# The second products' weight tiles 64 bytes further on in SBUF, in a fused attention and gated feed-forward kernel

## Chip, cores and metric

One NeuronCore of a Trainium2 chip runs the whole program. The metric is the device time of one execution in microseconds; a kernel's time is the median of several executions.

## The reference

Inputs are q, k, v of shape 8 x 8 x 576 x 64 (batch, heads, positions, head size) and three weight matrices. Attention is the sum of a coarse part (q, k, v averaged over groups of four positions, full softmax over 144 groups) and a band part (each position sees those at a distance under four). The result, seen as x of 4608 tokens by 512, goes through a normalisation and a gated feed-forward layer:

```python
rms = np.sqrt(np.mean(x * x, axis=-1, keepdims=True) + 1e-06)
xn = x / rms * rms_g
g = xn @ w_gate                         # 512 x 1536
silu = g * (1.0 / (1.0 + np.exp(-g)))
val = xn @ w_val                        # 512 x 1536
return (silu * val @ w_out)             # 1536 x 512
```

Everything is float32.

## The kernel before

The tokens are worked in 18 chunks (`c`) of 256. For every chunk the class `Attention` makes x: VectorE forms the band scores and most of the sums, ScalarE and GpSimd some of the products with v. `squares`, `mean`, `rms` and `root` give 1/rms, `norm` scales x, and `turn`, `high`, `low` turn it with TensorE and split it into `xh` (float32r) and the rest `xl`. The class `Coarse` does the coarse part for one pair of heads at a time, on TensorE too, spread over the program.

The class `Forward` does the feed-forward layer for a chunk, in 12 blocks `f` of 128 columns of w_gate and w_val. Weights too are kept as a float32r tile and its rest (`wg`, `wv`, `wo`, two of each), and each product is the sum of three: high by high, and high by rest both ways.

- `first(f, 0)` and `first(f, 1)` (L975) are 12 matmuls each. The stationary operand is a 128 x 128 piece of `wg` or `wv`, the moving operand 256 columns of `xh` or `xl`.
- `tanh`, `gate`, `product`, `high`, `low` turn the two results into `hs[f]` (its high part and its rest, each 256 wide).
- `second(f)` (L1010) is 6 matmuls that add to two output tiles. The stationary operand is a 128 x 128 piece of `hs`, the moving operand one block of `wo`, 512 columns. It follows `first` by `LAG` = 2 blocks.

So a block is 24 matmuls of 256 columns and 6 of 512; 18 x 12 blocks make 5184 and 1296 of them. Each matmul loads its stationary operand anew, and this load runs beside the matmul ahead of it.

All weights stay in SBUF in tiles of the pool `const`. Chunks 0 to 2, their weights, and the opening are put in order by a planner (`Plan`) with costs and due times; from chunk 3 on the program's order is written out in the loop at the end, and the tile framework lays the engines' queues out from it.

The tiles of one pool lie behind each other in the partition, in the order in which they are first asked for. Each weight class asks for its parts by need: `first_place` (blocks 0 to 7, which also serve as the first landing place of q, k and v sums), and `raw_place` (the last four blocks, as landing places of raw weights). The small tiles `z_b` (sums of the softmax, 64 bytes in a partition), `ss` (sums of squares, 32 bytes) and `rinv` (1/rms, 32 bytes) come from the pool `band`, two buffers each.

Of the kernel before, what the change touches and what calls it, by code (L numbers as in the profile page):

```python
# [8 lines left out]
FP32 = mybir.dt.float32  # L9
# [10 lines left out]
P = 128  # L20
# [13 lines left out]
US = 4  # L34
# [136 lines left out]
def attn_moe_kernel(  # L171
# [18 lines left out]
    const = ctx.enter_context(tc.tile_pool(name="const", bufs=1))  # L190
    stage = ctx.enter_context(tc.tile_pool(name="stage", bufs=1))
    loads = ctx.enter_context(tc.tile_pool(name="loads", bufs=2))
    band = ctx.enter_context(tc.tile_pool(name="band", bufs=2))
# [42 lines left out]
    wg = [Weight(f"wg{i}", [KT, P], [0, NF - 4, NF]) for i in range(2)]  # L236
    wv = [Weight(f"wv{i}", [KT, P], [0, NF - 4, NF]) for i in range(2)]
    wo = [Weight(f"wo{i}", [DM], [0, NF - 4, NF - 2, NF]) for i in range(2)]

# [343 lines left out]
    class Attention:  # L585
# [54 lines left out]
        def plan(self, newton="POOL", before=()):  # L640
# [69 lines left out]

            up_ready = [stored[b, hp] for p_ in {(2 * c + j) // UPP for j in range(2)} for b in (2 * p_, 2 * p_ + 1) for hp in range(KT)]
            squares, adds = [], []
            for j in range(2):
                load = task("ACT", 0.12, lambda j=j: self.load_up(j), T - 30, up_ready, allocs=[ups[j]], lag=2.5)
# [6 lines left out]
            self.added = adds  # L721
            mp = buf("ps_a")
            mean = task("PE", 0.2, self.mean, T - 10 - TAIL, squares, allocs=[mp])
            rms = task("DVE", 0.48, self.rms, T - 10, [mean], allocs=[r], uses=[mp])
            root = task(newton, 2.6 if newton == "POOL" else 1.9, lambda: self.root(newton), T - 10, [rms], uses=[r])
# [58 lines left out]
            nc.scalar.activation(out=self.f, in_=self.f, func=AF.Exp, scale=0.125)  # L784

        def total(self):
            self.z = band.tile([P, 4 * US], FP32, name="z_b")
            nc.vector.tensor_reduce(out=self.z, in_=self.f, axis=AX.X, op=ALU.add)

        def invert(self):  # L790
# [58 lines left out]

        def squares(self, j):  # L850
            if j == 0:
                self.ss = band.tile([P, 2 * US], FP32, name="ss")
            x = self.x[j].rearrange("p s t d -> p s (t d)")
            for s in range(US):
                nc.scalar.activation(
                    out=self.up[j].rearrange("p t d -> p (t d)"), in_=x[:, s], func=AF.Square,
                    accum_out=self.ss[:, j * US + s:j * US + s + 1],
                )
# [5 lines left out]
        def rms(self):  # L864
            self.r = band.tile([P, 2 * US], FP32, name="rms", bufs=1)
            nc.vector.tensor_scalar(
                out=self.r, in0=self.rp, scalar1=1.0 / DM, scalar2=1e-6, op0=ALU.mult, op1=ALU.add,
            )
            self.inv = band.tile([P, 2 * US], FP32, name="rinv")
            nc.vector.tensor_scalar(  # L870
                out=self.inv.bitcast(U32), in0=self.r.bitcast(U32), scalar1=1, scalar2=None, op0=ALU.logical_shift_right,
            )
            yi = self.inv.bitcast(U32)
            nc.vector.tensor_scalar(
                out=yi, in0=yi, scalar1=-1, scalar2=0x5F3759DF, op0=ALU.mult, op1=ALU.add,
            )
# [149 lines left out]
    for fg in range(3):  # L1026
        for i in range(12):
            if i % 3 == 2 if fg < 2 else i >= 8:
                f = 4 * fg + (i // 3 if fg < 2 else i - 8)
# [173 lines left out]
```

## Time and profile before

| | us |
|---|---|
| three timed runs, median | 1148.4 |
| their lowest and highest | 1146.32, 1149.47 |
| the profiled execution | 1145.97 |
| its span from first to last instruction | 1144.2 |
| TensorE busy in the span | 1082.0 |
| VectorE, ScalarE, GpSimd busy | 927.7, 624.1, 255.7 |
| mean granted TensorE clock | 0.977 |

TensorE's matmuls overlap: a matmul's record begins when it starts to stream and ends when its last result is out, so records of one engine lie over each other. How long one really takes from TensorE is the step from one start to the next, and is read from starts. A granted clock of 1.00 is 2.4 GHz, 0.50 is 1.2 GHz.

### The profile page before, as it was taken

What the parts mean: (1) busy time and instruction counts of PE and PEld (TensorE: products, weight loads), DVE (VectorE), ACT (ScalarE), POOL (GpSimd) and SP (SyncE); (2) the same over time, 40 slices, a digit from 0 to 9 for tenths busy, and PEclk for the clock granted to TensorE, in tenths of its full rate; (3) what the DMA queues carried; (4) which work ended last, traced back from release to release, by engine and by line L of the source; (5) the groups of instructions that cost most, each with busy time, mean ns of one, the idle gap of its engine ahead of it and who ended that gap; (6) DMA issues with size and microseconds to landing.
All of it is one profiled execution on the core that took longest, in us unless ns stands there. A gap on an engine that the chain in (4) does not pass through costs nothing.

```text
span 1144.2 us, 22238 instructions
## 1 busy us (share of the span) xinstructions
PE 1082.0 (95%) x8002; PEld 990.2 (87%) x8002; DVE 927.7 (81%) x1869; ACT 624.1 (55%) x2284; POOL 255.7 (22%) x317
## 2 busy tenths in 40 slices
PE   6883799999999899999999999999999999999998
PEld 4772698888899899999999999999999999999997
DVE  6787898778889989797979797979798989887432
ACT  1574673747392847474747474747475573837221
POOL 1554562334221211111111111101011020201000
PEclk9885999999999999999999999999999999999999
DMA  9985482446535353535263535222231313220000
GB/s 264 301 275 170 102 227 76 95 101 149 127 87 117 99 115 88 115 87 115 83 120 87 115 88 114 78 64 75 66 91 46 105 52 99 68 58 20 1 19 19
DMA packets 76815, 119.59 MB, mean 105 GB/s; under 512 B 26784, under 2 KB 36256, under 8 KB 76704
## 3 DMA queue, kind: packets, MB, share of 16 engines
q1 hardware_dynamic: 47520, 97.34, 28.8%
q0 software_dynamic: 8640, 15.93, 9.0%
q10 hardware_dynamic: 20544, 4.89, 2.0%
q8 instruction: 63, 1.03, 0.4%
q14 instruction: 48, 0.39, 0.1%
HBM read 106.33 MB, written 11.80 MB: 103 GB/s over the span
## 4 chain that ended last, share of the span: by engine, by line
PE 76%; DVE 9%; DMA 8%; ACT 3%; issue 3%; SPq 1%; POOL 1%; ACTq 0%; DVEq 0%; POOLq 0%
PE ps_h L975 46%; PE ps_o L1010 23%; PE ps_a L541 2%; DMA wg<-in_v_sum_dram 2%; DMA qk<-in_qk_sum_dram 2%; PE ps_a L499 2%; ACT prod L804 1%; DMA vs<-in_v_sum_dram 1%; PE ps_a L906 1%; DVE prod L757 1%; DVE o_sb L271 1%; PE ps_a L527 1%; DMA kv<-in_k_pad_dram 1%; DVE sc L761 1%; DMA up<-o_g 1%
## 5 line engine op out<-in xcount | busy, mean ns | idle before, releaser
L1010 PE MATMUL ps_o<-wo,hs 128*128 128x512 f32 x1296 | 356.0, 399 | 4.2 <-POOL hs L999 3.7
L975 PE MATMUL ps_h<-xh,wg 128*128 128x256 f32 x1728 | 348.2, 283 | 4.8 <-ACT xh L910 2.3
L975 PE MATMUL ps_h<-xh,wv 128*128 128x256 f32 x1728 | 343.0, 281 | 4.6 <-DVE sil L985 4.5
L975 PEld LDWEIGHTS ps_h<-xh,wg 128*128 128x128 f32 x1728 | 282.9, 190 | 14.2 <-ACT xh L910 3.0
L975 PEld LDWEIGHTS ps_h<-xh,wv 128*128 128x128 f32 x1728 | 281.9, 189 | 10.8 <-DVE sil L985 6.9
L804 ACT ACTIVATE prod<-kv,sc 128x64 f32<-128x64 f32 x1072 | 281.7, 408 | 13.0 <-DVE sc L795 4.8
L1010 PEld LDWEIGHTS ps_o<-wo,hs 128*128 128x128 f32 x1296 | 221.9, 188 | 41.4 <-POOL hs L999 6.2
L975 PE MATMUL ps_h<-xl,wg 128*128 128x256 f32 x864 | 244.8, 283 | 0.1
L975 PE MATMUL ps_h<-xl,wv 128*128 128x256 f32 x864 | 241.5, 280 | 0.0
L982 ACT ACTIVATE sil<-ps_h 128x256 f32<-128x256 f32 x216 | 82.9, 384 | 233.9 <-PE ps_h L975 208.8
L811 POOL TENSOR_TENSOR prod<-sc,kv 128x256 f32<-128x256 f32 x144 | 116.4, 843 | 397.4 <-DVE sc L795 175.4
L985 DVE SCALAR_TENSOR_TENSOR sil<-sil,ps_h 128x256 f32<-128x256 f32 x216 | 89.7, 415 | 103.1 <-ACT sil L982 91.0
L975 PEld LDWEIGHTS ps_h<-xl,wg 128*128 128x128 f32 x864 | 164.1, 190 | 6.9 <-issue 1.3
L975 PEld LDWEIGHTS ps_h<-xl,wv 128*128 128x128 f32 x864 | 163.6, 189 | 1.8
L996 ACT ACTIVATE hs<-sil 128x256 fp32r<-128x256 f32 x216 | 89.5, 416 | 136.9 <-DVE sil L990 122.4
L757 DVE TENSOR_TENSOR prod<-q_t,kv 128x896 f32<-128x896 f32 x140 | 151.7, 1086 | 5.6 <-DMA q_t<-in_q_band_dram 5.2
L830 DVE TENSOR_REDUCE x_t<-prod 128x128 f32<-128x896 f32 x128 | 136.8, 1077 | 23.6 <-ACT prod L804 16.4
L761 DVE TENSOR_REDUCE sc<-prod 128x14 f32<-128x896 f32 x144 | 154.5, 1077 | 0.4
L999 DVE TENSOR_TENSOR hs<-sil,hs 128x256 fp32r<-128x256 f32 x196 | 91.4, 466 | 29.5 <-ACT hs L996 29.2
L990 DVE SCALAR_TENSOR_TENSOR sil<-sil,ps_h 128x256 f32<-128x256 f32 x216 | 89.9, 416 | 8.1 <-PE ps_h L975 6.4
L362 POOL DMA_DIRECT2D qk<-in_qk_sum_dram x36 | 32.2, 895 | 187.3 <-DMA qk<-in_qk_sum_dram 111.8
L811 DVE TENSOR_TENSOR prod<-sc,kv 128x128 f32<-128x128 f32 (+2 forms) x144 | 69.5, 515 | 1.6 <-PE ps_o L826 0.8
(118 smaller groups left out, 984.3 us busy)
## 6 DMA issues: line engine op xcount, KB each, us to landing
kv<-in_k_pad_dram SPq DMA_DIRECT2D x72, 320.0 KB
kv<-in_v_pad_dram SPq DMA_DIRECT2D x72, 320.0 KB
qk<-in_qk_sum_dram POOLq DMA_DIRECT2D x36, 288.0 KB, 5.3
out_dram<-o_sb SPq DMA_DIRECT2D x36, 256.0 KB
q_t<-in_q_band_dram SPq DMA_DIRECT2D x70, 128.0 KB
vs<-in_v_sum_dram POOLq DMA_DIRECT2D x36, 144.0 KB, 3.5
qk<-in_qk_sum_dram SPq DMA_DIRECT2D x12, 288.0 KB
wo<-in_qk_sum_dram SPq DMA_DIRECT2D x2, 1152.0 KB
```

Of the source, the lines that this page charges most:

```text
L757: nc.vector.tensor_tensor(out=pr, in0=bcast(q[:, s0:s0 + 2], 2, NO), in1=window(k, s0), op=ALU.mult)
L761: nc.vector.tensor_reduce(out=self.sc[:, j, par, s0:s0 + 2], in_=self.pr[i], axis=AX.X, op=ALU.add,)
L804: nc.scalar.activation(out=self.pr[i][:, o, s], in_=self.v[j, par][:, s0 + s + o], func=AF.Copy, scale=p[:, s, o:o + 1],)
L811: (nc.vector if engine == "DVE" else nc.gpsimd).tensor_tensor(out=self.pr[i][:, a:b], in0=bcast(p[:, :, a:b].rearrange("p s o -> p o s"), ...
L830: nc.vector.tensor_reduce(out=self.x[j][:, s0:s0 + 2, par], in_=pr.rearrange("p o s d -> p s d o"), axis=AX.X, op=ALU.add,)
L975: nc.tensor.matmul(out=self.p[f][:, t], lhsT=wi(f)[:, 0, k], rhs=xi[:, k], start=(n == 0), stop=(n == 3 * KT - 1),)
L982: nc.scalar.activation(out=self.sil[f], in_=self.p[f][:, 0], func=AF.Tanh, scale=0.5)
L985: nc.vector.scalar_tensor_tensor(out=self.sil[f], in0=self.sil[f], scalar=1.0, in1=self.p[f][:, 0], op0=ALU.add, op1=ALU.mult,)
L990: nc.vector.scalar_tensor_tensor(out=self.sil[f], in0=self.sil[f], scalar=0.5, in1=self.p[f][:, 1], op0=ALU.mult, op1=ALU.mult,)
L996: nc.scalar.activation(out=self.hs[f][:, 0], in_=self.sil[f], func=AF.Copy)
L999: (nc.gpsimd if engine == "POOL" else nc.vector).tensor_tensor(out=self.hs[f][:, 1], in0=self.sil[f], in1=self.hs[f][:, 0], op=ALU.subtract,)
L1010: nc.tensor.matmul(out=self.o[j], lhsT=lhs[:, cols], rhs=rhs(f)[:, 0], start=(f == 0 and i == 0), stop=(f == NF - 1 and i == 2),)
```

## The change

The six small tiles become fixed tiles of the pool `const`, asked for between the weights, so that the weights are now laid out in a written order. Chunk `c` takes number `c % 2` of each, as the two buffers of the pool did.

```diff
+    small = {"ss": [const.tile([P, 2 * US], FP32, name=f"ss{i}") for i in range(2)]}
+    for w in wo:
+        w.first_place()
+    small["inv"] = [const.tile([P, 2 * US], FP32, name=f"rinv{i}") for i in range(2)]
+    for w in wg + wv:
+        w.first_place()
+    for w in wg + wv:
+        w.raw_place(1, 0)
+    small["z"] = [const.tile([P, 4 * US], FP32, name="z_b0")]
+    for k in (1, 2):
+        for w in wo:
+            w.raw_place(k, 0)
+    small["z"].append(const.tile([P, 4 * US], FP32, name="z_b1"))
...
-            self.z = band.tile([P, 4 * US], FP32, name="z_b")
+            self.z = small["z"][self.c % 2]
...
-                self.ss = band.tile([P, 2 * US], FP32, name="ss")
+                self.ss = small["ss"][self.c % 2]
...
-            self.inv = band.tile([P, 2 * US], FP32, name="rinv")
+            self.inv = small["inv"][self.c % 2]
```

No instruction is added, taken away or moved: every engine has the same instructions in the same order with the same waits and signals. Only addresses differ. In bytes from the partition's start, and what is left over 128:

| tiles | before | left over 128 | after | left over 128 |
|---|---|---|---|---|
| `wo`, blocks 0 to 7 (two) | 2432, 35200 | 0 | 2496, 18880 | 64 |
| `wo`, blocks 8 to 11 (four) | 133504 to 145792 | 0 | 133696 to 145984 | 64 |
| `wg`, `wv`, blocks 0 to 7 (four) | 18816 to 84352 | 0 | 35328 to 84480 | 0 |
| `wg`, `wv`, blocks 8 to 11 (four) | 100736 to 125312 | 0 | 100864 to 125440 | 0 |
| `raw`, `kv`, `q_t`, `up_t`, `sc`, `prod`, `m_b` | 149888 on | as after | 256 further on | as before |
| `x_t` | 175616, 177664 | 0 | 175744, 177792 | 0 |
| `z_b`, `ss`, `rinv`, `rms` | 175488 on | 0, 32, 64 or 96 | between the weights (`rms` 64 further on) | 0, 32, 64 or 96 |
| `xh`, `xl` (two each), `hs` (three), `sil`, `o_sb` and all others | 179904 on | 64 | not moved | 64 |

A row of 512 float32 columns is 2048 bytes and one of 256 is 1024, so what is left over 128 is the same at the start of every block and piece. Below, a tile with 0 left over is said to begin on the even half, one with 64 on the odd half. Before, `first` has its stationary operand on the even half and its moving one on the odd; `second` has its stationary operand (`hs`) on the odd half and its moving one (`wo`) on the even. After, both operands of `second` begin on the odd half, and `first` is as it was.

## Rows read from the trace of the kernel before

**Rows 1.** Part 1 of the page (busy time of each engine, its share of the span, instructions), and of part 2 the lines of TensorE and of its granted clock, in 40 slices of the span, in tenths.

```profile
PE 1082.0 (95%) x8002; PEld 990.2 (87%) x8002; DVE 927.7 (81%) x1869; ACT 624.1 (55%) x2284; POOL 255.7 (22%) x317
...
PE   6883799999999899999999999999999999999998
...
PEclk9885999999999999999999999999999999999999
```

**Rows 2.** Part 4 of the page, the chain of work that ended last, by engine and by line.

```profile
PE 76%; DVE 9%; DMA 8%; ACT 3%; issue 3%; SPq 1%; POOL 1%; ACTq 0%; DVEq 0%; POOLq 0%
PE ps_h L975 46%; PE ps_o L1010 23%; PE ps_a L541 2%; DMA wg<-in_v_sum_dram 2%; DMA qk<-in_qk_sum_dram 2%; PE ps_a L499 2%; ACT prod L804 1%; DMA vs<-in_v_sum_dram 1%; PE ps_a L906 1%; DVE prod L757 1%; DVE o_sb L271 1%; PE ps_a L527 1%; DMA kv<-in_k_pad_dram 1%; DVE sc L761 1%; DMA up<-o_g 1%
```

**Rows 3.** Of part 5 of the page the matmuls of `second` and the two groups of `first` on `xh`: number, busy time, mean length of a record, idle time ahead of them.

```profile
L1010 PE MATMUL ps_o<-wo,hs 128*128 128x512 f32 x1296 | 356.0, 399 | 4.2 <-POOL hs L999 3.7
L975 PE MATMUL ps_h<-xh,wg 128*128 128x256 f32 x1728 | 348.2, 283 | 4.8 <-ACT xh L910 2.3
L975 PE MATMUL ps_h<-xh,wv 128*128 128x256 f32 x1728 | 343.0, 281 | 4.6 <-DVE sil L985 4.5
```

**Rows 4.** TensorE by stretch: the stretch, its length, TensorE's busy time (matmul records that touch the stretch), granted clock, share of the DMA engines and GB/s.

```profile
390.00:1144.20 754.20, 749.85 (x5588) 1.00 0.31 77
420.00:1080.00 660.00, 660.00 (x4928) 1.00 0.32 80
```

**Rows 5.** The same for the matmuls of `second` (L1010) alone.

```profile
390.00:1144.20 754.20, 277.33 (x1008) 1.00 0.31 77
```

**Rows 6.** The same for the matmuls of `first` (L975) alone.

```profile
390.00:1144.20 754.20, 502.21 (x3954) 1.00 0.31 77
```

**Rows 7.** TensorE in order of time, one block near the end: start, length of the merged records, number. Left out are the other 256-column matmuls between: from 1104.07 there are 12 on `wg`, from 1105.46 there are 12 on `wv`, the last of them at 1106.70.

```profile
1104.07 0.28 PE L975 MATMUL ps_h<-xh,wg 128*128 128x256 f32 x1
...
1105.46 0.28 PE L975 MATMUL ps_h<-xh,wv 128*128 128x256 f32 x1
...
1106.70 0.28 PE L975 MATMUL ps_h<-xh,wv 128*128 128x256 f32 x1
1106.82 1.54 PE L1010 MATMUL ps_o<-wo,hs 128*128 128x512 f32 x6
1108.19 0.28 PE L975 MATMUL ps_h<-xh,wg 128*128 128x256 f32 x1
```

**Rows 8.** The loads of stationary operands at the border between `first` and `second` in the same block.

```profile
1106.59 0.19 PEld L975 LDWEIGHTS ps_h<-xh,wv 128*128 128x128 f32 x1
1106.71 1.21 PEld L1010 LDWEIGHTS ps_o<-wo,hs 128*128 128x128 f32 x6
1107.96 0.19 PEld L975 LDWEIGHTS ps_h<-xh,wg 128*128 128x128 f32 x1
```

**Rows 9.** TensorE in order of time, some 60 us earlier. Left out are the other 256-column matmuls: 12 on `wv` from 1042.42, 12 on `wg` from 1043.84, 4 on `wv` from 1045.25.

```profile
1042.42 0.28 PE L975 MATMUL ps_h<-xh,wv 128*128 128x256 f32 x1
...
1043.84 0.28 PE L975 MATMUL ps_h<-xh,wg 128*128 128x256 f32 x1
...
1045.25 0.28 PE L975 MATMUL ps_h<-xh,wv 128*128 128x256 f32 x1
...
1045.72 1.09 PE L1010 MATMUL ps_o<-wo,hs 128*128 128x512 f32 x4
1046.66 0.28 PE L975 MATMUL ps_h<-xl,wv 128*128 128x256 f32 x1
```

**Rows 10.** TensorE in order of time where `second` is split in four and two matmuls. Left out are 256-column matmuls: there are 5 from 1013.79, 7 from 1015.27, 6 from 1016.10, 6 from 1017.27 and 5 from 1017.97.

```profile
1013.79 0.28 PE L975 MATMUL ps_h<-xh,wg 128*128 128x256 f32 x1
...
1014.36 1.08 PE L1010 MATMUL ps_o<-wo,hs 128*128 128x512 f32 x4
1015.27 0.40 PE L975 MATMUL ps_h<-xh,wg 128*128 128x256 f32 x2
...
1016.10 0.28 PE L975 MATMUL ps_h<-xh,wv 128*128 128x256 f32 x1
...
1016.80 0.63 PE L1010 MATMUL ps_o<-wo,hs 128*128 128x512 f32 x2
1017.27 0.28 PE L975 MATMUL ps_h<-xh,wv 128*128 128x256 f32 x1
...
1017.97 0.28 PE L975 MATMUL ps_h<-xh,wg 128*128 128x256 f32 x1
...
1018.54 0.85 PE L1010 MATMUL ps_o<-wo,hs 128*128 128x512 f32 x3
```

**Rows 11.** TensorE in the opening: the last three of a group of products that keep TensorE at work while it waits (L1104, 256 columns, moving and stationary operand from the same tile `hs`), and the next product.

```profile
21.77 0.51 PE L1104 MATMUL ps_o<-hs 128*128 128x256 f32 x3
22.12 0.41 PE L408 MATMUL ps_h<-wo,ident_sb 128*128 128x288 f32 x1
```

**Rows 12.** Groups of instructions that write a moved small tile (VectorE) or a `wo` tile (ScalarE, GpSimd): number, busy time, mean ns of one, idle time ahead.

```profile
L788 DVE TENSOR_REDUCE z_b<-sc 128x16 f32<-128x112 f32 x18 | 4.7, 261 | 0.4 <-ACT sc L784 0.4
L874 DVE TENSOR_SCALAR rinv<-rinv 128x8 uint32<-128x8 uint32 x18 | 3.0, 164 | 0.1
...
L281 ACT CAST wo<-o_sb 128x512 fp32r<-128x512 f32 x12 | 7.4, 613 | 4.7 <-DVE o_sb L271 3.5 <-DVE sil L990 1.2
...
L291 POOL TENSOR_TENSOR wo<-o_sb,wo 128x512 fp32r<-128x512 f32 x10 | 15.7, 1566 | 27.4 <-ACT wo L281 27.3
```

## The prediction

> **What bounds the kernel now.** I read the page's busy times first, then the slices, the chain, the stretches, and last TensorE's own rows in order of time. TensorE is busy for 95% of the span [rows 1], and in the chain that ended last it holds 76%, `first` alone 46% and `second` 23% [rows 2]. The slices show where: TensorE is full from about the fourteenth on, and before that it waits in places [rows 1]. The stretch from 420 to 1080 us has not one idle moment on TensorE, and from 390 to the end 4.4 us of 754.2 are idle, at a granted clock of 1.00 [rows 4]. So from 390 us on, a nanosecond per matmul is a nanosecond per matmul of the result; before it, part of one is lost in waits that other engines end. This stretch holds 1008 of the 1296 matmuls of `second` [rows 3, 5] and 3954 of the 5184 of `first` [rows 6].
>
> What the reader is to see next is that the same matmul has two paces at the same clock. Near the end, twelve 256-column matmuls take 1106.82 - 1105.46 = 1.36 us, 113.3 ns each, and the six 512-column ones take 1.37 us, 228.3 each [rows 7]. Some 60 us earlier twelve take 1043.84 - 1042.42 = 1.42 us, and the next twelve 1.41, so 118 each, and four of 512 columns take 0.94 us, 235 each [rows 9]. Call these the fast and the slow pace. The switch between them is sharp, and it happens at `second`: five matmuls of `first` run at 114 ns, four of `second` at (1015.27 - 1014.36)/4 = 227.5, and then seven of `first` at 118.6 and six more at 117; after two of `second` at 235, six more take 0.70 us at 117, and then five are back at 114 [rows 10]. Even in the fast blocks something is left behind: the twelve on `wg` right after `second` take 1105.46 - 1104.07 = 1.39 us, 0.03 more than the twelve on `wv` [rows 7]. A whole fast block lasts 1108.19 - 1104.07 = 4.12 us, where 36 times 113.3 ns would be 4.08 [rows 7].
>
> **The change, part by part.** Nothing is added or moved in any queue, so the sum has no term from an instruction's number, place or wait. What is left is the price of an address.
>
> *The small tiles.* Instructions on `z_b` and `rinv` are 18 to a group and 164 to 261 ns each on VectorE [rows 12]. Their two buffers alternate as before. I take nothing for them: the cover is TensorE, which has no idle moment beside them in 420 to 1080 us [rows 4]. Without that cover, even a tenth more on the two groups shown would be 0.8 us in all, (4.7 + 3.0)/10.
>
> *Writing the `wo` tiles.* Twelve casts of 613 ns on ScalarE and ten subtractions of 1566 ns on GpSimd [rows 12], once, in the planned opening. A tenth more would be 0.7 and 1.6 us, on engines that are not full there; I take nothing, and 2 us as the upper bound.
>
> *`first`.* Its operands stay on the halves where they were. Its price can move only through what `second` leaves behind.
>
> *`second`.* Here the moving operand goes to the odd half, where the moving operand of `first` is already, and comes to share a half with its own stationary operand. The trace has no 512-column matmul of that kind, so the bounds are the nearest rows. Below: 2 x 113.3 = 226.7 ns, the fast pace of `first`, which streams from the odd half. Above: 235 ns, the slow pace that `second` itself has [rows 9]; a 256-column product that takes both operands from one tile, so from the same half, steps at (22.12 - 21.77)/3 = 117 ns [rows 11], which is 234 for 512 columns. As the present mean I take 231, between 228.3 and 235. The bounds are then -4.3 us and +4.0 us for 1008 matmuls, and I lean to the lower one, for this reason: in a block, five of the six borders between like matmuls keep their halves, and the one from `first` to `second` and the one back change the half of the moving operand; the leftover of 0.03 us stands right behind such a border [rows 7], and so do the switches of pace [rows 10]. After the change the moving operand never changes its half at these borders. Against the fear that the shared half costs much speaks the load of `hs` at 1106.71 [rows 8]: it runs beside the last matmul of `first`, whose moving operand is on the same half, and that matmul still steps 0.12 us [rows 7].
>
> The sum, against the profiled execution. 3954/24 is 165 blocks from 390 us on. I take half of them as fast, since the mean records of the two groups of `first`, 283 and 281 ns, do not lean clearly to either pace [rows 3]. 82 fast blocks by 4.12 - 4.08 = 0.04 us: -3.3 us. Of the slow ones I take a quarter, 20, as made slow by a split `second` as in [rows 10]; they would stay fast, 24 matmuls by 118 - 113.3 = 4.7 ns: -2.2 us. Together -5.5 us, from 1145.97 to about 1140.5. The profiled execution lies 2.4 us under the median of the timed runs, so the same step from the median is 1148.4 - 5.5 = 1142.9. I forecast 1143 us.
>
> A rule of the Trainium skill speaks against this. "SBUF — State Buffer", section "Who interferes with whom", gives TensorE two read ports of its own for the moving and the stationary operand and says that it never waits on anyone; by that an address costs nothing and the sum is 0, 1148.4. The trace does not bear out the plain form of it: at one clock the same matmul steps at 113.3 or at 118 ns.
>
> Another page gives a lower floor. By "TensorE: Matmul & The Clock Gate", section "Back-to-back issue gap", an isolated gap is N/2.4 + 2.5 ns, 215.8 for 512 columns; an estimate from it, 231 - 215.8 over 1008 matmuls, would be -15 us. No row here shows 512 float32r columns in that time.
>
> **The rivals.** *No change to speak of.* The two paces may be a matter of when matmuls start against each other, and not of where they read. For it: the same addresses, in the same order, give both paces [rows 7, 9], and the load on the shared half costs its neighbour nothing [rows 8]. Against it: `second` keeps a leftover that `first`, in its own rows, does not have. Time: 1148.4, give or take 2 us. This is also the case in which the change does not do what moving the tiles could do.
>
> *Slower.* Moving and stationary operand of `second` on one half get in each other's way, at every load. For it: the product with both operands on one half steps at 117 ns, not 113.3 [rows 11]; against it, these are three steps in the opening, with transfers about, and the one load of [rows 8]. Price: `second` at 235 instead of 231, +4.0 us; and `first` enters its slow pace after it and stays there, as it does in [rows 10], in the 82 blocks that are fast now: 24 x 4.7 ns less the leftover of 0.03 us is 0.083 us each, +6.8 us. Together 1148.4 + 10.8 = 1159. It decides where `first` does not come back to 113 ns within the twelve matmuls behind `second`; if it does come back, +4.0 alone stays, 1152.
>
> *Faster by more.* All of `first` at the fast pace: about 82 slow blocks by 24 x 4.7 ns = 0.113 us, -9.3, with -4.3 for `second`: 1134.8. Against it: the coarse part and the transposes stand between blocks too and also disturb the pace, and they do not change.
>
> **How the numbers follow.** About 0.3%, 3.4 us, is what a measurement of this kernel tells from no change. The forecast, with the little that goes beyond it, I give 0.43; no change 0.35; slower 0.22. The likeliest one's own range is 1138 to 1146. For the range to hold 8 in 10 it must take in no change and the mild form of slower, and most of the way to all-fast: 1136 to 1154. Left out are the full slower case and the last bit of all-fast.
>
> **What would show it.** In the changed kernel's rows in order of time near the end: six matmuls of `second` in 1.36 us instead of 1.37, and the twelve on `wg` behind them in 1.36 instead of 1.39, a block in 4.08. Where `second` is split in four and two, `first` should stay at 113 to 114 ns. If blocks still last 4.12 us and the split still switches the pace, addresses do not matter and the rival without change holds. If the six take 1.41 us or `first` stays at 118 behind them, the shared half costs. Wrong altogether would be the forecast if TensorE's stretch from 420 to 1080 us got idle time, since that would mean that another engine pays for its tiles' new places.

## The result, and the profile after

The changed kernel takes 1154.9 us (median of six, 1153.48 to 1156.85) against 1148.4 us, a ratio of 1.0057 with a 95% interval of 1.0039 to 1.0075. It is 0.6% slower, where a gain of about 0.5% was forecast: 1143 us, in a range of 1136 to 1154, which misses it by one microsecond. The profiled execution took 1154.22 us, with a span of 1152.5 us. Its line numbers are 16 higher: `first` is L991, `second` is L1026.

From the page after: busy times, and the groups of matmuls that answer [rows 3].

```profile
PE 1091.9 (95%) x8002; PEld 999.1 (87%) x8002; DVE 924.9 (80%) x1869; ACT 624.0 (54%) x2284; POOL 259.2 (22%) x317
...
L1026 PE MATMUL ps_o<-wo,hs 128*128 128x512 f32 x1296 | 356.9, 399 | 3.2 <-POOL hs L1015 2.7
L991 PE MATMUL ps_h<-xh,wg 128*128 128x256 f32 x1728 | 351.7, 283 | 4.7 <-ACT xh L926 2.3
L991 PE MATMUL ps_h<-xh,wv 128*128 128x256 f32 x1728 | 348.6, 282 | 4.4 <-DVE sil L1001 4.3
```

The busy times of the vector, scalar and gpsimd engines differ from [rows 1] by 3.5 us at most, TensorE's by 9.9, and the idle time ahead of these matmuls is no longer than in [rows 3]. What grew is busy TensorE, above all `first`, the product whose price I had left alone: its two groups on `xh` rose by 3.5 and 5.6 us, `second` by 0.9.

TensorE by stretch: stretch, length, busy time (matmul records that touch it), granted clock, share of the DMA engines, GB/s. The first row is the opening before, the second the opening after, the third the answer to [rows 4].

```profile
0.00:390.00 390.00, 332.16 (x2416) 0.93 0.59 157
0.00:390.00 390.00, 333.73 (x2411) 0.92 0.59 157
420.00:1080.00 660.00, 660.00 (x4884) 1.00 0.32 80
```

In the same 660 us without an idle moment, at the same clock, 4884 matmuls touch the stretch instead of 4928. At 660/4928 = 0.134 us each those 44 are 5.9 us. The two profiled spans, 1144.2 and 1152.5, differ by 8.3 us. Five matmuls, 0.7 us of it, are lost in the first 390 us. The order of the matmuls is the same in both traces, so each has its partner. By these partners 7.6 us are lost after 390 us: 6.3 in the steps within `first`, 1.1 in those within `second`, and 0.2 in all others.

One block near the end, the answer to [rows 7]: start, length of the merged records, number. Twelve matmuls on `wg` begin at 1107.52, twelve on `wv` at 1108.93; the other 256-column matmuls are left out.

```profile
1106.14 1.54 PE L1026 MATMUL ps_o<-wo,hs 128*128 128x512 f32 x6
1107.52 0.28 PE L991 MATMUL ps_h<-xh,wg 128*128 128x256 f32 x1
...
1108.93 0.28 PE L991 MATMUL ps_h<-xh,wv 128*128 128x256 f32 x1
...
1110.34 1.54 PE L1026 MATMUL ps_o<-wo,hs 128*128 128x512 f32 x6
1111.72 0.28 PE L991 MATMUL ps_h<-xh,wg 128*128 128x256 f32 x1
```

The 24 matmuls of `first` take 1110.34 - 1107.52 = 2.82 us, 117.5 ns each, where they took 1106.82 - 1104.07 = 2.75 us in [rows 7]; the six of `second` take 1.38 us against 1.37. A block is 4.20 us against 4.12.

Below I count the steps from one start to the next of the same line, at full clock. Before, 2404 steps of `first` are at 115 ns or less and 2181 at 116 to 119. After, 336 and 4291. The mean step goes from 115.65 to 117.51 ns in `first` and from 230.47 to 231.68 in `second`. So the slow pace of [rows 9, 10], which held `first` for about half of the time, now holds it nearly always.

### The profile page after: what moved, and what is told of

It reads as the page before. It is cut to its first block, busy times and chain, and to the rows that moved or that the text cites. A ratio compares the mean times of both kernels' runs of the same rounds, so it can differ in the third digit from the quotient of the medians.

```text
span 1152.5 us, 22238 instructions
## 1 busy us (share of the span) xinstructions
PE 1091.9 (95%) x8002; PEld 999.1 (87%) x8002; DVE 924.9 (80%) x1869; ACT 624.0 (54%) x2284; POOL 259.2 (22%) x317
## 4 chain that ended last, share of the span: by engine, by line
PE 82%; DVE 7%; DMA 5%; ACT 2%; issue 2%; SPq 1%; POOL 0%; ACTq 0%; DVEq 0%; POOLq 0%
PE ps_h L991 50%; PE ps_o L1026 24%; PE ps_a L557 2%; PE ps_a L515 2%; DMA wg<-in_v_sum_dram 2%; DMA qk<-in_qk_sum_dram 1%; PE ps_a L922 1%; PE ps_a L543 1%; DVE o_sb L287 1%; DMA vs<-in_v_sum_dram 1%; ACT prod L820 1%; PE ps_a L842 1%; DVE prod L773 1%; ACT up_t L871 1%; DVE sc L777 1%
## 5 line engine op out<-in xcount | busy, mean ns | idle before, releaser
L1026 PE MATMUL ps_o<-wo,hs 128*128 128x512 f32 x1296 | 356.9, 399 | 3.2 <-POOL hs L1015 2.7
L991 PE MATMUL ps_h<-xh,wg 128*128 128x256 f32 x1728 | 351.7, 283 | 4.7 <-ACT xh L926 2.3
L991 PE MATMUL ps_h<-xh,wv 128*128 128x256 f32 x1728 | 348.6, 282 | 4.4 <-DVE sil L1001 4.3
L991 PEld LDWEIGHTS ps_h<-xh,wg 128*128 128x128 f32 x1728 | 283.2, 189 | 14.0 <-ACT xh L926 3.0
L991 PEld LDWEIGHTS ps_h<-xh,wv 128*128 128x128 f32 x1728 | 283.0, 189 | 10.5 <-DVE sil L1001 6.6
L1026 PEld LDWEIGHTS ps_o<-wo,hs 128*128 128x128 f32 x1296 | 221.8, 188 | 41.8 <-POOL hs L1015 5.3
L991 PE MATMUL ps_h<-xl,wg 128*128 128x256 f32 x864 | 245.4, 284 | 0.2 <-DVE xl L930 0.2
L991 PE MATMUL ps_h<-xl,wv 128*128 128x256 f32 x864 | 242.7, 281 | 0.0
L991 PEld LDWEIGHTS ps_h<-xl,wg 128*128 128x128 f32 x864 | 163.6, 189 | 7.1 <-issue 1.7
L991 PEld LDWEIGHTS ps_h<-xl,wv 128*128 128x128 f32 x864 | 163.3, 189 | 1.8
```

The costliest lines, as they stand in the source:

```text
L991: nc.tensor.matmul(out=self.p[f][:, t], lhsT=wi(f)[:, 0, k], rhs=xi[:, k], start=(n == 0), stop=(n == 3 * KT - 1),)
L1026: nc.tensor.matmul(out=self.o[j], lhsT=lhs[:, cols], rhs=rhs(f)[:, 0], start=(f == 0 and i == 0), stop=(f == NF - 1 and i == 2),)
```

## What the experiments asked

The change moves two things that my prediction looked at over 128 bytes only. Over 512 bytes, `wg` and `wv` go from 384 to 0: they too are moved, by 128 bytes. `wo` goes from 384 to 448 in blocks 0 to 7 only. In blocks 8 to 11, which lie behind `z_b0`, it goes from 384 to 64 (133504 to 133696), which is 192 bytes and not 64; the remainder of 64 over 128 hides this. `xh`, `xl` and `hs` stay at 320. I give the **distance** of a product, the start of its moving operand less that of its stationary one, over 256 bytes: for `first` 320 - 384, which is 192, becomes 320 - 0, which is 64; for `second` it goes from 64 to 128, and to 0 in blocks 8 to 11.

Every kernel below issues the program's own matmuls in the same order. The four probes add a tail of dummy matmuls behind them, whose results nobody reads; of these kernels only the steps in the tail count.

| kernel | wg, wv | wo | hs | distance first, second | time over before [95%] | `first` steps to 115 / 116 to 119 ns | matmuls in 420:1080 |
|---|---|---|---|---|---|---|---|
| before | 384 | 384 | 320 | 192, 64 | 1 | 2404 / 2181 | 4928 |
| the change | 0 | 448, 64 in blocks 8 to 11 | 320 | 64, 128 or 0 | 1.0057 [1.0039, 1.0075] | 336 / 4291 | 4884 |
| wo_odd | 384 | 448 | 320 | 192, 128 | 1.0021 [0.9988, 1.0055] | 1920 / 2646 | 4906 |
| wg_128 | 0 | 384 | 320 | 64, 64 | 1.0061 [1.0046, 1.0076] | 353 / 4262 | 4884 |
| order_only | 384 | 384 | 320 | 192, 64 | 0.9981 [0.9967, 0.9996] | 2519 / 2071 | 4926 |
| order_again | 384 | 384 | 320 | 192, 64 | 0.9995 [0.9971, 1.0018] | 2516 / 2070 | 4930 |
| wg_256 | 128 | 384 | 320 | 192, 64 | 1.0005 [0.9987, 1.0022] | 2527 / 2021 | 4930 |
| wo_192 | 384 | 64 | 320 | 192, 0 | 1.0026 [1.0006, 1.0046] | 1615 / 3071 | 4907 |
| hs_wo_192 | 384 | 64 | 384 | 192, 192 | 0.9978 [0.9959, 0.9998] | 3234 / 1467 | 4945 |
| hs_wo_128 | 384 | 0 | 384 | 192, 128 | 0.9947 [0.9926, 0.9969] | 3835 / 810 | 4966 |

The places are bytes over 512. Each time stands over that of executions of before taken beside the kernel. The last two columns are from each kernel's profiled execution, and but for the first timing of order_only they tell what the time tells: 22 matmuls fewer at 0.134 us are 2.9 us, 0.26% of 1148, beside 0.21% measured for wo_odd, whose interval takes in 1; 38 more are 5.1 us, 0.44%, beside 0.53% for hs_wo_128.

## The change taken apart: wo_odd, wg_128, order_only

The pieces of code below are shortened, and their signs stand against the changed kernel. Only `wo` moved, with all small tiles fixed (`wg` and `wv` are asked for first and stay at 384). Here all blocks of `wo` are at 448; no run has `wo` in the two places of the change with `wg` and `wv` left at 384:

```diff
-    small = {"ss": ...}
-    for w in wo: w.first_place()
-    small["inv"] = ...
     for w in wg + wv: w.first_place()
     for w in wg + wv: w.raw_place(1, 0)
+    small["ss"] = ...
+    for w in wo: w.first_place()
...
```

> The wo tiles on the odd half (64 left over 128), as in the change; wg and wv keep what they had before over 512 bytes (384), where the change had moved them to 0 over 512. The small tiles are fixed, the order of the weights in the partition is wg, wv, wo. Theory H (the shared half of second's two operands throws first into its slow pace): first at 118 ns nearly throughout, time about 1155, a ratio of 1.005 to 1.006 to before. Theory W (it was the 128 bytes by which wg and wv moved too, that is first's own operands): first as mixed as before, time about 1148.

Only `wg` and `wv` moved (`wo` asked for first, at 384; small tiles of 128 bytes in all behind it, then `wg` and `wv` at 0):

```diff
-    small = {"ss": ...}
     for w in wo: w.first_place()
+    for k in (1, 2):
+        for w in wo: w.raw_place(k, 0)
+    small["ss"] = ...
     small["inv"] = ...
     for w in wg + wv: w.first_place()
...
```

> wo stays on the even half, at 384 over 512 as before; wg and wv lie at 0 over 512 as in the change (on the even half still). Theory H: time as before, 1148, and first mixed between 113 and 118 ns. Theory W: first at 118 ns nearly throughout, about 1155.

Neither moved: `wo`, then `wg` and `wv`, and all six small tiles behind them.

> All weights at 384 over 512, as before; only the small tiles are fixed ones (behind the weights), the order of the weights in the partition is that of a written list, and raw, kv, prod and x_t lie where the change put them. Theories H and W both: as before, 1148, ratio 0.998 to 1.002. If the small tiles, the order of the weights or the tiles behind them were the cause: 1155.

The stretch from 420 to 1080 us in wo_odd and then in wg_128, to be held against 4928 in [rows 4]:

```profile
420.00:1080.00 660.00, 660.00 (x4906) 1.00 0.32 81
```

```profile
420.00:1080.00 660.00, 660.00 (x4884) 1.00 0.32 81
```

The move of `wg` and `wv` alone is the whole loss: 1.0061, the same 4884 matmuls, and 353 of 4615 steps at the better pace beside the change's 336 of 4627. A move of all of `wo` by 64 bytes, nearly the one that names the change, costs 22 matmuls in the trace, and its time of 1.0021 cannot be told from no change. The two do not add up: in wg_128 `first` is at the worse pace nearly always already. Order and small tiles cost nothing: from 420 to 1080 us order_only steps as before does, matmul by matmul, with 8 of 4925 steps off by more than 2 ns and their sum the same to 0.01 us. The gain of 0.2% in the first timing of order_only was not there in a second one of twelve executions:

> The change without its moves of the weights: the six small tiles are fixed and lie behind all weights, and the weights lie in the written order, all at 384 over 512 as before. An earlier timing gave 0.9981 of the time before, with an interval of 0.9967 to 0.9996. If order and small tiles cost nothing, and the first reading was the edge of its interval, this gives 0.998 to 1.001 with 1 inside the interval; if the order is a gain of its own, 0.997 to 0.999 again with 1 outside.

It gave 0.9995 with 1 well inside the interval, so there is no gain of the order that could be told.

## Which remainder counts: probe_halves, probe_fine, wg_256

> The kernel before, and behind its last block a row of matmuls of the shapes of first and second alone, on weight tiles, with chosen places over 512 bytes; they add about 290 us to the time and nobody reads their results. First 36 matmuls of 256 columns for each place of the stationary operand, the moving one at 320; then 18 of 512 columns for six pairs of places; then five blocks of 24 and 6 for nine sets of places, those of before and of the change among them. Theory H: the 256-column ones alone take 113 ns while the two operands lie on different halves and 118 on the same; the blocks with the places of the change last 4.2 us (first slow), those of before 4.12, and those with wo alone moved 4.2. Theory W: the set with wo alone moved lasts 4.12, the set with wg alone moved 4.2. If places do not matter at all, all sets last the same.

The tail's first part in order of time: 36 matmuls of 256 columns for each place of the stationary operand, with the moving one at 320. From L1163 on the places are 384, 448, 0, 64, 128, 192, 256, 320. The last row is the start of the next trial.

```profile
1146.19 4.43 PE L1166 MATMUL ps_h<-wv,wg 128*128 128x256 f32 x36
1150.45 4.40 PE L1169 MATMUL ps_h<-wv,wg 128*128 128x256 f32 x36
1154.69 4.48 PE L1172 MATMUL ps_h<-wv,wg 128*128 128x256 f32 x36
1159.01 4.26 PE L1175 MATMUL ps_h<-wv,wg 128*128 128x256 f32 x36
1163.11 4.43 PE L1178 MATMUL ps_h<-wv,wg 128*128 128x256 f32 x36
1167.38 4.40 PE L1181 MATMUL ps_h<-wv,wg 128*128 128x256 f32 x36
1171.62 4.48 PE L1184 MATMUL ps_h<-wv,wg 128*128 128x256 f32 x36
1175.94 0.52 PE L1187 MATMUL ps_h<-wv,wg 128*128 128x256 f32 x3
```

Start to start over 36: 448 gives (1150.45 - 1146.19)/36 = 118.3 ns, 0 gives 117.8, 64 gives 120, 128 gives 113.9, 192 gives 118.6, 256 gives 117.8 and 320 gives 120. So 0 and 128 differ, which my halves of 128 bytes called alike, and 0 and 256 agree, as do 64 and 320. In this trial the period is 256. Blocks of 24 and 6 from the same tail, first with the places of before (L1211, L1213), then with those of the change (L1216, L1218; `wo` at 448):

```profile
1213.73 2.91 PE L1211 MATMUL ps_h<-wv,wg 128*128 128x256 f32 x24
1216.48 1.54 PE L1213 MATMUL ps_o<-wo,wv 128*128 128x512 f32 x6
1217.85 0.40 PE L1211 MATMUL ps_h<-wv,wg 128*128 128x256 f32 x2
...
1234.42 2.99 PE L1216 MATMUL ps_h<-wv,wg 128*128 128x256 f32 x24
1237.25 1.54 PE L1218 MATMUL ps_o<-wo,wv 128*128 128x512 f32 x6
1238.62 0.64 PE L1216 MATMUL ps_h<-wv,wg 128*128 128x256 f32 x4
```

1217.85 - 1213.73 = 4.12 us and 1238.62 - 1234.42 = 4.20 us: the blocks of [rows 7] and of the kernel after, made without any of the program around them. In this tail the other engines do nothing. The row gives the stretch, its length, the busy time of TensorE, of its loads, of VectorE, ScalarE and GpSimd, then clock, share of the DMA engines and GB/s:

```profile
1195.00:1395.00 200.00, 200.00 (x1388) 185.99 (x1387) 0.00 (x0) 0.00 (x0) 0.00 (x0) 1.00 0.00 1
```

So the two paces need neither transfers nor other engines; TensorE's own operands and the order of its matmuls are enough. Of the other sets in this tail, the blocks with `wo` alone moved settle at 4.14 us and those with `wg` alone moved at 4.22, as theory W has it.

If the period is 256, another 128 bytes under `wg` and `wv` must bring the time back. This kernel is wg_128 with the 128 bytes of `z` ahead of `wg` too:

> wo as before; wg and wv 256 bytes over 512 on from where they were (128 where they had 384), twice as far as in the change. Theory W256: first as mixed as before, ratio to before 0.997 to 1.003. If any move of wg and wv costs, or if the period is 512 bytes: first at 118 ns throughout, 1.005 to 1.007.

```profile
420.00:1080.00 660.00, 660.00 (x4930) 1.00 0.33 82
```

It does: 4930 matmuls in the stretch and 1.0005. Matmul by matmul, from 420 to 1080 us, 8 of 4925 steps are off from before's by more than 2 ns; in wg_128 it is 2412. This is the run that settles which part of the change loses, since between wg_128 and wg_256 nothing differs but the addresses of `wg` and `wv` and of the two `z_b`. The 7.1 us by which its profiled span is longer than before's, 1151.3 against 1144.2, all lie ahead of 420 us, where TensorE waits in places.

> The kernel before, and behind its last block matmuls alone as in the run before, nobody reads them. 36 matmuls of 256 columns for each distance between the starts of the moving and the stationary operand from 0 to 240 over 256 bytes in steps of 16, the moving operand fixed; five more at distance 192 with the moving operand elsewhere; 18 of 512 columns for each of the same 16 distances; then five blocks with the places of before but wo 192 bytes on (twice, with wg once 256 bytes off), and of before. Theory W256 (the pace is set by the distance of the two operands' starts over 256 bytes): 256 columns at 113.3 ns only near 192, at 117 to 120 elsewhere; 512 columns at 226.7 only near 0, 233 elsewhere; a block with wo 192 bytes on lasts 4.08 to 4.10 us, with wg 256 bytes off as well. Theory of halves (128 bytes): distances 128 apart have the same pace.

In steps of 16 bytes no distance gave 256 columns under 116.5 ns, and 192 itself came out at (1200.63 - 1196.39)/36 = 117.8, where the first probe's stationary 128, also at 192, had locked in at 113.3:

```profile
1196.39 4.40 PE L1199 MATMUL ps_h<-wv,wg 128*128 128x256 f32 x36
1200.63 4.30 PE L1202 MATMUL ps_h<-wv,wg 128*128 128x256 f32 x35
...
1301.05 2.88 PE L1274 MATMUL ps_h<-wv,wg 128*128 128x256 f32 x24
1303.77 1.55 PE L1276 MATMUL ps_o<-wo,wv 128*128 128x512 f32 x6
1305.15 2.99 PE L1274 MATMUL ps_h<-wv,wg 128*128 128x256 f32 x24
1307.98 1.55 PE L1276 MATMUL ps_o<-wo,wv 128*128 128x512 f32 x6
```

Five more trials at distance 192, with the moving operand elsewhere, gave 113.8, 117.8, 113.8, 117.8 and 113.7 in turn. The lower rows, blocks with the places of before but `wo` 192 bytes on, say why one address has no one price. The same 24 matmuls take 1303.77 - 1301.05 = 2.72 us (113.3 ns), and after six of `second` 1307.98 - 1305.15 = 2.83 us (117.9), and stay so. The block of 4.08 to 4.10 us that I expected was there once, 1305.15 - 1301.05; later ones take 4.21, with `wg` 256 bytes off too. Of 512 columns, only distances 0 and 240 settle at 226.7 ns; the others take 230.8 to 234.3. That made me try distance 0 for `second`, in the full kernel wo_192 (all small tiles but one between `wg`, `wv` and `wo`, so `wo` at 64):

> wg and wv as before (384 over 512); all wo tiles at 64 over 512, 192 bytes on, where they start at the same place over 256 bytes as hs. Theory W256: second at 226.7 to 229 ns a matmul instead of 231, -2 to -4 us, and first no worse than before, since its operands stay at their distance; time 1142 to 1147, ratio 0.995 to 1.000. Theory of halves (wo on the odd half is bad for what follows): like the change or the run with wo alone moved by 64 bytes, 1.002 to 1.006.

This missed: 1.0026, and only 1615 steps of `first` at the better pace. The rows above show the reason in small: the place that is best for `second` by itself leaves `first` in the worse pace behind it.

## What decides the pace: probe_entry and probe_scan

> The kernel before with a tail of matmuls that nobody reads, so only the steps of the tail count. It tells whether the pace of the first products at the places of before (moving operand at 320 over 512, stationary at 384) depends on what ran ahead of them. Ahead of each trial stand twelve 256-column matmuls with the stationary operand at 0, which is the change's place and keeps 117.8 ns. Then 36 matmuls at the places of before follow: at once; behind six, four and two 512-column matmuls at the places of before; behind six with the moving operand at 64; behind twelve with the stationary operand at 128. Theory of two stable paces (T2): the 36 run wholly at about 113.3 or wholly at about 117.8 ns, and which one is set by what stands ahead of them; at once behind the slow ones 117.8, behind six of 512 columns 113.3, behind four 117.8. Rival, an address has one pace and the rest is drift over time (T1): all six trials within 0.5 ns of one value. Then blocks of 24 and 6 as in the program, with the places of before for the first products and eight other places for the second products' weights, and five blocks with all operands of the first products 64 bytes further on: T2 expects most of these to come out near 4.20 us, the places of before again 4.12; a set under 4.10 would be a layout that beats both kernels.

In order of time, with the places as the expectation gives them. L1166, L1172, L1178, L1184, L1190 are the twelve at the change's place; L1170, L1176, L1182, L1188, L1194 the 36 at the place of before; L1168, L1174, L1180, L1186 are of 512 columns, and L1192 the twelve with the stationary operand at 128. The last row is the start of the blocks behind the trials.

```profile
1144.27 1.52 PE L1166 MATMUL ps_h<-wv,wg 128*128 128x256 f32 x12
1145.63 1.54 PE L1168 MATMUL ps_o<-wo,wv 128*128 128x512 f32 x6
1147.01 4.27 PE L1170 MATMUL ps_h<-wv,wg 128*128 128x256 f32 x36
1151.11 1.52 PE L1172 MATMUL ps_h<-wv,wg 128*128 128x256 f32 x12
1152.47 1.08 PE L1174 MATMUL ps_o<-wo,wv 128*128 128x512 f32 x4
1153.39 4.40 PE L1176 MATMUL ps_h<-wv,wg 128*128 128x256 f32 x36
1157.63 1.57 PE L1178 MATMUL ps_h<-wv,wg 128*128 128x256 f32 x12
1159.04 0.62 PE L1180 MATMUL ps_o<-wo,wv 128*128 128x512 f32 x2
1159.50 4.25 PE L1182 MATMUL ps_h<-wv,wg 128*128 128x256 f32 x36
1163.58 1.52 PE L1184 MATMUL ps_h<-wv,wg 128*128 128x256 f32 x12
1164.94 1.55 PE L1186 MATMUL ps_o<-wo,wv 128*128 128x512 f32 x6
1166.33 4.41 PE L1188 MATMUL ps_h<-wv,wg 128*128 128x256 f32 x36
1170.57 1.57 PE L1190 MATMUL ps_h<-wv,wg 128*128 128x256 f32 x12
1171.98 1.52 PE L1192 MATMUL ps_h<-wv,wg 128*128 128x256 f32 x12
1173.34 4.24 PE L1194 MATMUL ps_h<-wv,wg 128*128 128x256 f32 x36
1177.42 0.84 PE L1197 MATMUL ps_h<-wv,wg 128*128 128x256 f32 x6
```

The 36 take 4.10 us behind six of 512 columns (1147.01 to 1151.11, 113.9 ns), 4.24 behind four (117.8), 4.08 behind two (113.3), 4.24 behind six from another place (117.8), and 4.08 behind twelve with the stationary operand at 128 (113.3). One pace with a drift is out: what stands ahead decides. The first of the six trials tells nothing, since six matmuls of the program fell into it. Of the other five each ran once, and the number of 512-column matmuls is not told apart from the pace ahead of them, which was the worse one before the two and the better one before the six and the four.

Half of my setup was wrong, though, and this is the better lesson. The twelve at the change's place were to run at 117.8 always. They take 1145.63 - 1144.27 = 1.36 us, 113.3 ns, behind 36 at that pace, and 1.41 behind 36 at the other. So distance 64 can hold either pace too. What the places decide is whether the matmuls come back to the better pace, or are put out of it, at a border between products. The program's own rows say the same: from 390 us on, `first` comes back to the better pace at 42 of the 65 borders made of `second` alone that it reaches at the worse one in the kernel before, and at 1 of 131 after the change.

The same tail ran thirteen more sets of places as blocks of 24 and 6. I had expected most to take near 4.20 us and hoped for one under 4.10. Six settled at 4.20 to 4.23, six at 4.11 to 4.15, one went to and fro, and none settled under 4.10.

> The kernel before with a tail of matmuls that nobody reads; only the tail's steps count. For 30 sets of places it runs one and the same pattern of 252 matmuls of 256 columns and 48 of 512, in the order in which the program itself mixes them (whole blocks, and second products split in four and two). Two theories on what the change lost. If the loss comes from how the first products leave the slow pace behind the second products, the pattern lasts longest with the change's places (about 252 x 117.7 + 48 x 231 = 40.7 us), and with the places of before between that and the floor of 252 x 113.3 + 48 x 226.7 = 39.4 us, at about 40.2. If a set of places has one pace, splits or not, the places of before give 252 x 113.4 + 48 x 229 = 39.6. From the blocks measured before, the weights of the second products 16 bytes ahead of their place before (distance 48) should be the best or near it, 39.7 to 40.0, and the worst ones 40.9.

The pattern has 228 and 42 matmuls, not the 252 and 48 that the expectation counts with; by its paces the change's places should take 228 x 117.7 + 42 x 231 = 36.54 us, and the floor is 228 x 113.3 + 42 x 226.7 = 35.35. Starts of three neighbouring patterns: places of before, of the change, and `second` at distance 0. Behind them, further on, those of the places that hs_wo_128 and hs_wo_192 below have, and the next start.

```profile
1147.40 1.21 PE L1170 MATMUL ps_o<-wo,wv 128*128 128x512 f32 x4 [0.44 <-ACT o_sb L1017]
...
1183.37 1.10 PE L1179 MATMUL ps_o<-wo,wv 128*128 128x512 f32 x4
...
1219.91 1.10 PE L1188 MATMUL ps_o<-wo,wv 128*128 128x512 f32 x4
...
2013.31 1.09 PE L1386 MATMUL ps_o<-wo,wv 128*128 128x512 f32 x4
...
2048.98 1.09 PE L1395 MATMUL ps_o<-wo,wv 128*128 128x512 f32 x4
...
2084.62 0.62 PE L1404 MATMUL ps_o<-wo,wv 128*128 128x512 f32 x2
```

Before 1183.37 - 1147.40 = 35.97 us (a second time, further on, 35.85), the change 36.54, as worked out. Splits and all, the scan puts the layouts in nearly the order of the program: `wo` at 448 with `wg` at 384 took 36.26, and `wo` at 320, which is 64 over 256 as in wo_192, 36.27. The best sets took 35.63 to 35.67 (2048.98 - 2013.31 is one of them) with 208 to 225 of 228 matmuls at the better pace, the places of before 154 and 151. All operands moved by 64 bytes together made no difference: two sets took 35.64 and 35.67, and with that move 35.64 and 35.66. One of the best, `wo` at 368, needs places in steps of 16 bytes, and tiles come in steps of 32; two others move `hs` by 64 bytes and `wo` to 64 or to 0, and those I ran.

## A layout that beats both: hs_wo_192 and hs_wo_128

The small tiles again make the room, and one tile of 64 bytes at the head of the pool `ffn` moves `hs` (and `sil` and `o_sb`) by 64. This is hs_wo_128, where both `z_b` stand ahead of `wo`; in hs_wo_192 `ss`, `rinv` and one `z_b` do:

```diff
+    for w in wg + wv: w.first_place()
+    for w in wg + wv: w.raw_place(1, 0)
+    small["z"] = ...
+    for w in wo: w.first_place()
...
+    ffn.tile([P, 16], FP32, name="pad", bufs=1)
```

> The change without its move of wg and wv, and with two other places: wo at 64 over 512 and, by a tile of 64 bytes at the head of their pool, hs at 384 instead of 320. First products then stand at the distance of before, 192 over 256, second products at 192 too (64 - 384). In the scan of patterns this set took 35.64 us against 35.97 and 35.85 for the places of before, with 218 of 228 matmuls of 256 columns at 113 ns instead of 154. Theory P, the state in which the second products leave TensorE sets the pace of the first: 5184/228 = 22.7 patterns by 0.27 us give -6 us, 0.995 (0.992 to 0.997), and over four fifths of the first products at 115 ns or less. Rival Q, the scan's tail isn't the program (other matmuls, waits and transfers stand between, and the opening isn't full): 0.998 to 1.002 with a share of fast first products near the 55% of before.

> The same with wo at 0 over 512 instead of 64, so a distance of 128 (0 - 384) in the second products and still 192 in the first. In the scan 35.67 us, 220 of 228 fast. Theory P: 0.995 (0.992 to 0.997), as its neighbour, and both alike within 0.002. Rival Q: 0.998 to 1.002. Distance 128 in the second products is also what the change had; so with first products at distance 192 it isn't the distance in the second products alone that loses.

The stretch in hs_wo_128, for which before has 4928:

```profile
420.00:1080.00 660.00, 660.00 (x4966) 1.00 0.32 81
```

hs_wo_128 takes 1143.3 us and 0.9947 of before [0.9926, 0.9969], with 83% of the counted steps of `first` at the better pace: as its theory had it. hs_wo_192 has 69% and 0.9978, a gain that falls short of that theory, and the two are not alike. `second` got dearer on the way, 233.9 ns in hs_wo_128 against 230.5: matmul by matmul, from 420 to 1080 us, it gives back 2.2 us of the 6.7 that the steps within `first` win.

hs_wo_128 and wo_odd have the same two distances, 192 and 128, and lie on either side of before, with 4966 and 4906 matmuls in the stretch against 4928. So a distance within each product does not settle it; how the addresses of `second` stand to those of `first` counts too. Which relation it is, the runs do not tell.

## Why the prediction was wrong

- **The bound was right.** TensorE had no idle moment in 420 to 1080 us before or after, the other engines did not matter, and nanoseconds per matmul became microseconds of the result.
- **The two paces were right**, as was the guess that half of `first` ran at each (2404 to 2181 steps), and that the switch happens at `second`: before, from 390 us on, 75 of 76 changes of pace from one row of `first` to the next stand at borders made of `second` alone.
- **The step that failed is the one on `first`**: "Its operands stay on the halves where they were. Its price can move only through what `second` leaves behind." The operands do stay over 128 bytes. Over 256 bytes `wg` and `wv` moved by half a period, and wg_128 and wg_256 show that this is the loss. The front table had the addresses, and I looked at their remainder over 128 without a row that shows that period. A term that I put at nothing measured +6.3 us from 390 us on, and by the mean steps +1.86 x 5184 = +9.6 us over the whole program, an upper figure, since in the opening TensorE waits.
- **The gain in the sum**, -3.3 us for fast blocks and -2.2 for slow ones, did not come: a block near the end went from 4.12 to 4.20 us, and the pace behind a split stayed the worse one.
- **The term of `second`** was leaned to -4.3 us, of which the sum took only what the fast blocks hold. By the mean steps it is +1.2 x 1296 = +1.6 us, inside the bounds, on the other side. Its own places are not needed for that: in wg_128, where `wo` and `hs` stay, its mean step is 231.6 ns as well.
- **The near miss of the range is luck.** Its upper end was set for `second` alone getting dearer, not for what happened to `first`.
- **The leftover of 0.03 us behind `second`** I read as a price of changing halves. In the probes it is a way back: in the blocks with the places of before three to five matmuls at 116 to 124 ns, and then 113.3. After the change that way back is not taken.
- **The rival that ended slower** had the mechanism, `first` at the worse pace behind `second` and staying there, and named a cause that the runs do not bear out: both operands of `second` on one half. wg_128 leaves `second` where it was and loses all. The rival's 1159 was 4 us over; its chance had been put at 0.22.
- **No change to speak of** held that addresses do not matter. wg_256 against wg_128 refutes it: an address alone moved the time by 0.6%. With it falls what I had read out of the Trainium skill, "SBUF — State Buffer", section "Who interferes with whom": from its rule that TensorE never waits on anyone I took that an address costs nothing. The rule itself is not refuted, since the two paces show in tails where every other engine is idle.

Not settled: what inside the chip makes the two paces, and why the one way back exists at some places and not at others. No run here looks into that.

## To carry over

When a change moves one tile, list the address of every operand that it pushes along, and compare at more than one period, since the loss here came from tiles that the change did not mean to move. Where one matmul has two paces at one clock, don't price the addresses of one product alone: run the program's own mix of products as a tail of dummy matmuls, splits and all, for many layouts in one execution. Here such a scan ranked the layouts nearly as the full kernels did and found one that gained 0.5%.

## What had not been expected of the hardware

- The step of a matmul depends on where its operands begin. In the trial of 64-byte steps and in the full kernel wg_256 the period is 256 bytes. Over a trial the mean step was 113.7 to 120 ns for 256 columns, and it settled at 226.7 to 234.3 ns for 512, at a granted clock of 1.00.
- At one and the same pair of places both 113.3 and 117.8 ns are kept over 36 matmuls, and the matmuls ahead decide which.
- A split of `second` works both ways: before, from 390 us on, four matmuls of 512 columns alone turned the better pace of `first` into the worse one 24 times of 24, and the worse into the better 18 times of 30.
- With the starts of its operands the same over 256 bytes, TensorE repeats its steps from kernel to kernel: from 420 to 1080 us, 8 of 4925 steps of order_only, order_again and wg_256 are off from before's by more than 2 ns.
